# Block sums of the down-projection's weights moved wholly to GpSimd, and the tail's load ring laid over the masked exponentials

## The chip, the cores and the metric

The kernel runs on one core of one Trainium2 chip. Its engines are TensorE (PE, matrix products), VectorE (DVE), ScalarE (ACT), GpSimd (POOL) and SyncE (SP, which here only issues DMAs). Each works through its own list of instructions in order; semaphores join them. The metric is the time of one execution on the device, in microseconds, as the median of several runs.

## The reference

Inputs are x (2048 rows, D = 512), attention weights, the weights of a SwiGLU layer of width F = 1792, and a gate vector. All is float32.

```python
g = sigmoid((x * gate_w).sum(-1, keepdims=True))
# a: 32 heads of 16; a query sees itself and the 255 keys before it
scores = where(mask, q @ k.T * 16 ** -0.5, -1e9)
a = (softmax(scores) @ v).transpose(0, 2, 1, 3).reshape(1, 2048, 512) @ wo
b = (silu(x @ w_gate) * (x @ w_up)) @ w_down
return g * a + (1 - g) * b
```

## The kernel before

**Precision.** A float32 operand is split into a high part (rounded to the type f32r that TensorE reads) and the remainder, the low part; each product is three matmuls (high x high, low x high, high x low). The helper `split` does it: a copy makes the high part, a subtraction (L73) the low part. In the main loop ScalarE mostly makes the high parts (L70) and GpSimd the low ones.

**Main loop.** The attention runs over 8 groups of 4 heads (g) and 16 blocks of 128 positions (i): 128 t-steps, t = 16 g + i, each with four turns hd = 0 to 3, one per head. In a turn TensorE makes a first score product for the row maxima of the next group (L302, reduced by VectorE at L304), a second score product of the present group (L341), whose exponential ScalarE takes (L343), and three steps of the dense projections (`lanes`, L252: gate, up and the next q and k halves). GpSimd masks each pair of exponentials with two selects, L345 and L348, into tiles `pt` of the pool `ptp`. At t%4 == 0, turn 1, the attention product of the four blocks before is made (`av`, L365): it reads the masked `pt` of the step before it. Its result is evicted by ScalarE (L380), transposed and normalised by VectorE, and stored by GpSimd's queue to `od` in DRAM (L395); the tiles of this (`o`) lie in the pool `osb`.

**Order.** There is no automatic scheduler here: the order is written out by hand. `later(t, hd, f)` puts a function into a table AT, and the loop calls what stands at (t, hd) at the end of that turn. The position in this table is the position in the list of the engine that executes it, masks and exponentials of the turn included. SyncE's list holds nearly all loads and stores: the stacked q and k halves, the values (`vg`), weights (`raw`), results kept for later (`kept_h`).

**Block sums.** The down projection runs in the tail in a form with seven block products in place of eight (Winograd's), over the halves of F and of D. It needs four sums of the blocks of the weights `wd`. `sums(k)`, L668 to L693, makes them for k = 0 to 6, once in each of the first seven groups: load two blocks (L674) into a pair of buffers, four additions in place of 128x256 each on GpSimd (L680), two copies 128x512 that make the high parts (L684, ScalarE), two subtractions that make the low parts (L688, GpSimd), and two stores to `sd` in DRAM (L691), which the tail reads. Its inner `at(n, ...)` turns a slot number n, in turns counted from the start of group k, into a place in AT. The pair of buffers comes from `x_pair()`; there is only one pair (bufs=1), which the halves of the next q and k projections (`group_half`, written at L70 by ScalarE and L73 by GpSimd) and the gate (`gate_place`) use in turn. For odd k the next user comes at t+8 of the group.

**Tail.** Behind the loop TensorE makes the last tile of gate and up (`last_tile`, L790; ScalarE's tanh L793 and VectorE make the product), then the output projection of the attention (`mm3`, L88 to L90, with `wo` and `od`) and the seven block products. Loads come through the pool `got` with 10 buffers (`taken`, L757 to L760; L759 issues), split tiles through `hp`, to which the tiles `sg` of the tanh belong. Both pools are opened where `ptp` and `osb` have been closed, in the same memory: pools on the right side grow from that end in the order in which they are opened.

Of the kernel before, what the change touches and what calls it, by code (L numbers as in the profile page):

```python
# [9 lines left out]
F32 = mybir.dt.float32  # L10
# [14 lines left out]
NP = NF // 2  # L25
HD = D // 2
# [10 lines left out]
def gated_mix(ctx, tc, xT, xn, wqk, wv, wo, wgu, wd, gw, outT):  # L37
# [4 lines left out]
    nc = tc.nc  # L42
# [65 lines left out]
    def halves_of(t):  # L108
        n = t.shape[-1] // 2
        return [t[:, :n], t[:, n:]]  # L110
# [43 lines left out]
    sd = dram.tile([4, P, NP, 2, HD], F32, name="sd")  # L154
# [46 lines left out]
    with ExitStack() as A:  # L201
# [19 lines left out]
        def x_pair(pool=None, name="x"):  # L221
            return tuple((pool or sm).tile([P, 2 * CH], F32R, name=f"{name}{w}", bufs=1) for w in ("hi", "lo"))
# [291 lines left out]
        for n, turn in enumerate(turns):  # L514
            for m, _ in enumerate(turn, 3 * NK * n):
                at = [max(0, i - wait) * 2 * NB // (total - wait) for i in (m, m + 1)]
# [19 lines left out]
        def later(t, hd, *fs):  # L536
            AT.setdefault((t, hd), []).extend(fs)

        for n, key in enumerate(KEYS[:-1]):
            if n:  # L540
                t, free = FIRST[key], LAST.get(KEYS[n - 2], 0) + 1 if n > 1 else 0
# [112 lines left out]
        for b in range(NB):  # L654
            t, hd = blocks[b]
            later(t, hd, lambda b=b: gate_block(b))
            if b > 1:
                t, hd = blocks[b - 2]
# [9 lines left out]
        def sums(k):  # L668

            t, buf = k * NB, []  # L670

            def load():
                buf.extend(x_pair())
                nc.sync.dma_start(buf[1].bitcast(F32).rearrange("p (m c) -> p m c", m=2), wd[k:k + NP + 1:NP].rearrange("m p c -> p m c"))  # L674

            def add(m):
                a11, a21, a12, a22 = (buf[1][:, r * HD:(r + 1) * HD].bitcast(F32) for r in range(4))
                to, x, y, op = ((a22, a21, a22, ALU.add), (a21, a11, a21, ALU.subtract),
                                (a11, a22, a11, ALU.subtract), (a12, a12, a11, ALU.subtract))[m]
                nc.gpsimd.tensor_tensor(out=to, in0=x, in1=y, op=op)  # L680

            def high():
                for hi, lo in zip(*map(halves_of, buf)):
                    nc.scalar.copy(hi, lo.bitcast(F32))  # L684

            def low(m):
                hi, lo = (halves_of(t)[m] for t in buf)
                nc.gpsimd.tensor_tensor(out=lo, in0=lo.bitcast(F32), in1=hi.bitcast(F32), op=ALU.subtract)  # L688

            def store(h):  # L690
                nc.sync.dma_start(sd[:, :, k, h].rearrange("j p c -> p j c"),  # L691
                                  buf[h].bitcast(F32).rearrange("p (j c) -> p j c", c=HD))
            def at(n, f, *args):  # L693
                n += 20 + (0 if k % 2 else 3) + (k == NP - 1)
                later(t + n // 4, n % 4, lambda: f(*args))
            later(t + 3, 0, load)
            for m in range(4):
                at(m, add, m)
            at(4, high)
            at(5, store, 0)  # L700
            for m in range(2):
                at(5 + m, low, m)
            at(6, store, 1)

        for k in range(NP):
            sums(k)
# [5 lines left out]
        for t in range(G * NB + 1):  # L712
# [6 lines left out]
            for hd in range(4):  # L719
# [10 lines left out]
                if hd == 1 and part == 0:  # L730
                    if t:
                        ag, c = divmod(d - 1, NCH)
# [11 lines left out]


    with ExitStack() as B:
        hp = B.enter_context(tc.tile_pool(name="hp", bufs=LEAD + 2, side="right"))
        got = B.enter_context(tc.tile_pool(name="got", bufs=10, side="right"))
        wop = B.enter_context(tc.tile_pool(name="wop", bufs=1))

        woh = wop.tile([P, NK, D], F32R, name="woh")
# [2 lines left out]
        def column():  # L754
            return hp.tile([P, CH], F32, name="sg", bufs=4)
# [211 lines left out]
        store = last_tile(0)  # L967
# [15 lines left out]
        store = last_tile(2)  # L983
# [14 lines left out]
        at = {e: n for n, e in enumerate(ITEMS)}  # L998
# [7 lines left out]
        for j in range(2 * NP):  # L1006
            two = divmod(j, 2)
            n = WO + j
# [10 lines left out]
        for n, e in enumerate(ITEMS[:end]):  # L1019
# [13 lines left out]
            p, k, pr = e  # L1033
# [7 lines left out]
        for d in range(2):  # L1041
            t = column()
# [38 lines left out]
```

## Time and profile before

| | |
|---|---|
| median of 3 runs | 829.19 us (828.38 to 829.83) |
| the profiled execution | 835.47 us, its span 833.8 us |
| mean granted clock of TensorE in it | 0.99 |
| busy in the span | PE 810.1, DVE 609.1, ACT 434.2, POOL 378.8 us |

How to read the lines shown below: a timeline row gives start, duration (both us), engine, line of the kernel, operation, output and input by their names in the program, the shapes, and in brackets how long the engine was idle before it and on what. A row of waits gives the engine and instruction that waited, what ended it, the sum in us, how often, and the longest. A row of windows gives a stretch of time, its length, the busy time (and count) of PE, PE's weight loads, DVE, ACT and POOL, then the granted clock as a fraction, the share of the DMA engines' time in use, and GB/s. A group's row gives the count, then the busy sum in us and the mean in ns of one, then the idle time before. Times count from the start of the span.

### The profile page before, as it was taken

The page shows a single profiled execution, that of the slowest core. Times are in us where ns is not written, and L with a number is a line of the kernel's source. Part 1 is how long each engine was busy: PE and PEld are TensorE (multiplying, and loading weights), DVE is VectorE, ACT ScalarE, POOL GpSimd, SP SyncE. Part 2 cuts the span into 40 slices and gives each one's busy share as a digit, 9 for nine tenths or more (in the row PEclk, how much of TensorE's full clock was granted, in tenths as well). Part 3 has the DMA queues.
Part 4 walks back from the last instruction along what each step waited for, and adds up shares of the span by engine and source line. Part 5 has one row for each costly group of instructions (what it writes and reads, how often), then busy time and mean ns, then how long its engine had stood idle before and what let it go on. Part 6 is the DMA issues. An engine that isn't in the chain of part 4 may idle for free. (4 is left out here: it accounts for less than half of the span.)

```text
span 833.8 us, 21474 instructions
## 1 busy us (share of the span) xinstructions
PE 810.1 (97%) x8251; PEld 682.3 (82%) x8251; DVE 609.1 (73%) x1641; ACT 434.2 (52%) x882; POOL 378.8 (45%) x689
## 2 busy tenths in 40 slices
PE   8999999999999999999998999899999989999997
PEld 7888988878878888887887888678887768888886
DVE  5396767768876887787775778786664455898975
ACT  6423556565555566555655566545642323554441
POOL 7722466575556467546656555545640021000112
PEclk9999999999999999999998999999999999999999
DMA  8583525444253364363445416544626699248535
GB/s 290 163 243 118 159 104 143 125 150 146 78 184 103 109 190 149 105 181 115 131 125 165 138 41 203 153 146 141 221 92 208 231 318 328 72 162 265 101 58 95
DMA packets 68378, 130.26 MB, mean 156 GB/s; under 512 B 11124, under 2 KB 23924, under 8 KB 68020
## 3 DMA queue, kind: packets, MB, share of 16 engines
q1 hardware_dynamic: 61172, 107.66, 42.4%
q0 software_dynamic: 7104, 21.24, 8.7%
q8 instruction: 65, 1.06, 0.5%
q14 instruction: 37, 0.30, 0.1%
HBM read 60.16 MB, written 43.53 MB: 124 GB/s over the span
## 5 line engine op out<-in xcount | busy, mean ns | idle before, releaser
L304 DVE CUSTOM_DVE_ANT_0 ps<-ps,mask 128x384 f32<-128x384 f32 (+2 forms) x512 | 268.8, 540 | 113.0 <-PE ps L302 54.8
L343 ACT ACTIVATE pt<-ps 128x384 f32<-128x384 f32 (+2 forms) x512 | 237.3, 474 | 134.5 <-PE ps L302 70.6
L345 POOL TENSOR_SCALAR_AFFINE_SELECT pt<-pt 128x256 f32<-128x256 f32 x256 | 109.8, 430 | 184.0 <-ACT pt L343 182.5
L341 PE MATMUL ps<-q,k 64*128 64x384 f32 (+2 forms) x512 | 162.8, 337 | 11.2 <-ACT pt L343 11.0
L302 PE MATMUL ps<-k,q 63*128 63x384 f32 (+2 forms) x512 | 160.4, 333 | 1.5 <-DVE mx L304 1.5
L252 PE MATMUL pb<-xhi,wh 64*128 64x512 f32 x512 | 117.6, 400 | 0.2
L252 PE MATMUL pb<-xlo,wh 64*128 64x512 f32 x512 | 114.9, 394 | 0.0
L252 PE MATMUL pb<-xhi,wl 64*128 64x512 f32 x512 | 114.7, 394 | 0.0
L252 PE MATMUL pa<-xhi,wh 64*128 64x512 f32 x512 | 114.2, 396 | 0.0
L252 PE MATMUL pa<-xlo,wh 64*128 64x512 f32 x512 | 112.8, 393 | 0.0
L252 PE MATMUL pa<-xhi,wl 64*128 64x512 f32 x512 | 112.6, 393 | 0.0
L341 PEld LDWEIGHTS ps<-q,k 64*128 64x128 f32 x512 | 91.3, 186 | 19.5 <-ACT pt L343 14.9
L302 PEld LDWEIGHTS ps<-k,q 63*128 63x128 f32 x512 | 89.4, 186 | 20.4 <-DVE mx L304 5.8
L348 POOL TENSOR_SCALAR_AFFINE_SELECT pt<-pt 128x256 f32<-128x256 f32 x224 | 95.7, 427 | 0.0
L365 PE MATMUL ps<-pt,vg 64*32 64x320 f32 (+4 forms) x1408 | 75.0, 346 | 0.0
L365 PE MATMUL pb<-pt,vg 64*32 64x320 f32 (+3 forms) x1360 | 73.9, 350 | 0.1
L304 DVE DVE_READ_ACCUMULATOR2_ANT mx<- 128x1 f32 x512 | 71.7, 140 | 0.0
L365 PEld LDWEIGHTS pb<-pt,vg 64*32 64x32 f32 x1360 | 46.4, 106 | 28.4 <-DVE mx L304 5.2
L252 PEld LDWEIGHTS pb<-xhi,wh 64*128 64x128 f32 x512 | 61.2, 187 | 7.0 <-DVE o L382 1.6
L252 PEld LDWEIGHTS pb<-xhi,wl 64*128 64x128 f32 x512 | 61.4, 186 | 5.2
L252 PEld LDWEIGHTS pa<-xhi,wl 64*128 64x128 f32 x512 | 59.3, 185 | 5.8
L252 PEld LDWEIGHTS pa<-xhi,wh 64*128 64x128 f32 x512 | 59.4, 187 | 3.9
(271 smaller groups left out, 1651.1 us busy)
## 6 DMA issues: line engine op xcount, KB each, us to landing
kept_h<-ev SPq DMA_DIRECT2D x52, 256.0 KB
od<-o POOLq DMA_DIRECT2D x32, 256.0 KB, 3.5
raw<-wgu SPq DMA_DIRECT2D x28, 256.0 KB
q<-xhi SPq DMA_DIRECT2D x56, 128.0 KB
k<-xhi SPq DMA_DIRECT2D x56, 128.0 KB
outT<-sg POOLq DMA_DIRECT2D x28, 256.0 KB, 4.7
vd<-vs POOLq DMA_DIRECT2D x8, 672.0 KB, 4.6
vg<-vd SPq DMA_DIRECT2D x32, 168.0 KB
```

What stands on the lines that cost most here:

```text
L252: mm = nc.tensor.matmul(ps[me], w[r], x[r], start=not second and i == 0, stop=bool(second) and i == n - 1)
L302: nc.tensor.matmul(ps[:, :n], QT[g % 2][pr][r, q0:q0 + P], KT[g % 2][pr][r, k0:k0 + n], start=True, stop=True)
L304: mx = nc.vector.tensor_tensor_reduce(out=ps[:, :n], in0=ps[:, :n], in1=mask[:, 3 * P - n:], scale=1.0, scalar=NEG, op0=ALU.add, op1=ALU.m ...
L341: nc.tensor.matmul(ps[:, :n], KT[g % 2][pr][r, k0:k0 + P], QT[g % 2][pr][r, k0:k0 + n], start=True, stop=True)
L343: BEHIND.append(nc.scalar.activation(pt[:, j, :n], ps[:, :n], AF.Exp, scale=SCALE))
L345: nc.gpsimd.affine_select(out=pt[:, :, :P], in_=pt[:, :, :P], pattern=[[0, 2], [1, P]], compare_op=ALU.is_ge, fill=0.0, base=0, channel_mu ...
L348: nc.gpsimd.affine_select(out=pt[:, :, 2 * P:], in_=pt[:, :, 2 * P:], pattern=[[0, 2], [-1, P]], compare_op=ALU.is_ge, fill=0.0, base=-1, ...
L365: nc.tensor.matmul(AV[g, c][h][32 * j:32 * j + 32, q0 - c * CH:q1 - c * CH], VG[4 * g + kb // 4][o, kb % 4, 17 * j:17 * j + 32], PT[g, kb, ...
```

## The change

Three things change. In `sums`, the load and both stores are issued on GpSimd's queue in place of SyncE's, and the two copies are made by GpSimd in place of ScalarE. The table of slots changes with it: additions now start at slot 24 for even k and 22 for odd k (before 23 and 20, one more for the last k), the load four slots ahead of them (before at slot 12), the copies and the first subtraction stand together, each store behind its subtraction. In the tail, `got` is opened ahead of `hp`, so that the loads' ring lies over the memory of the masked exponentials, and the `hp` tiles where the ring's last buffers lay, over `o`.

```diff
@@ -671,7 +671,7 @@
 
             def load():
                 buf.extend(x_pair())
-                nc.sync.dma_start(buf[1].bitcast(F32).rearrange("p (m c) -> p m c", m=2), wd[k:k + NP + 1:NP].rearrange("m p c -> p m c"))
+                nc.gpsimd.dma_start(buf[1].bitcast(F32).rearrange("p (m c) -> p m c", m=2), wd[k:k + NP + 1:NP].rearrange("m p c -> p m c"))
 
             def add(m):
                 a11, a21, a12, a22 = (buf[1][:, r * HD:(r + 1) * HD].bitcast(F32) for r in range(4))
@@ -681,26 +681,27 @@
 
             def high():
                 for hi, lo in zip(*map(halves_of, buf)):
-                    nc.scalar.copy(hi, lo.bitcast(F32))
+                    nc.gpsimd.tensor_copy(hi, lo.bitcast(F32))
 
             def low(m):
                 hi, lo = (halves_of(t)[m] for t in buf)
                 nc.gpsimd.tensor_tensor(out=lo, in0=lo.bitcast(F32), in1=hi.bitcast(F32), op=ALU.subtract)
 
             def store(h):
-                nc.sync.dma_start(sd[:, :, k, h].rearrange("j p c -> p j c"),
-                                  buf[h].bitcast(F32).rearrange("p (j c) -> p j c", c=HD))
+                nc.gpsimd.dma_start(sd[:, :, k, h].rearrange("j p c -> p j c"),
+                                    buf[h].bitcast(F32).rearrange("p (j c) -> p j c", c=HD))
+
             def at(n, f, *args):
-                n += 20 + (0 if k % 2 else 3) + (k == NP - 1)
+                n += 22 + 2 * (k % 2 == 0)
                 later(t + n // 4, n % 4, lambda: f(*args))
-            later(t + 3, 0, load)
+            at(-4, load)
             for m in range(4):
                 at(m, add, m)
             at(4, high)
-            at(5, store, 0)
             for m in range(2):
-                at(5 + m, low, m)
-            at(6, store, 1)
+                at(4 + m, low, m)
+            for h in range(2):
+                at(5 + h, store, h)
 
         for k in range(NP):
             sums(k)
@@ -744,8 +745,8 @@
 
 
     with ExitStack() as B:
+        got = B.enter_context(tc.tile_pool(name="got", bufs=10, side="right"))
         hp = B.enter_context(tc.tile_pool(name="hp", bufs=LEAD + 2, side="right"))
-        got = B.enter_context(tc.tile_pool(name="got", bufs=10, side="right"))
         wop = B.enter_context(tc.tile_pool(name="wop", bufs=1))
 
         woh = wop.tile([P, NK, D], F32R, name="woh")
```

On GpSimd, at the block sum k=2, from the last addition to the pair of masks whose end the attention product at t=40 awaits. Before (`pt` are the masked exponentials, `wl` the low part of a projection's weights):

```order
L680 TENSOR_TENSOR xlo<-xlo 128x256
L345 AFFINE_SELECT pt<-pt 128x2x128
L348 AFFINE_SELECT pt<-pt 128x2x128
L688 TENSOR_TENSOR xlo<-xlo,xhi 128x512
L73 TENSOR_TENSOR wl<-raw,wh 128x512
L345 AFFINE_SELECT pt<-pt 128x2x128
L348 AFFINE_SELECT pt<-pt 128x2x128
L688 TENSOR_TENSOR xlo<-xlo,xhi 128x512
L345 AFFINE_SELECT pt<-pt 128x2x128
L348 AFFINE_SELECT pt<-pt 128x2x128
```

After:

```order
L680 TENSOR_TENSOR xlo<-xlo 128x256
L684 CAST xhi<-xlo 128x512 x2
L688 TENSOR_TENSOR xlo<-xlo,xhi 128x512
L73 TENSOR_TENSOR wl<-raw,wh 128x512
L345 AFFINE_SELECT pt<-pt 128x2x128
L348 AFFINE_SELECT pt<-pt 128x2x128
L688 TENSOR_TENSOR xlo<-xlo,xhi 128x512
L691 DMA sd<-xhi 128x4x256
L691 DMA sd<-xlo 128x4x256
L345 AFFINE_SELECT pt<-pt 128x2x128
L348 AFFINE_SELECT pt<-pt 128x2x128
```

Two copies have come ahead of the subtractions and two stores behind them, all ahead of the awaited pair, the last row of both.

On GpSimd, at the block sum k=1, up to the masks that the attention product at t=24 awaits and the next write to the buffers (`xlo<-ev,xhi`). Before:

```order
L348 AFFINE_SELECT pt<-pt 128x2x128
L688 TENSOR_TENSOR xlo<-xlo,xhi 128x512
L395 DMA od<-o_1347 128x512
L688 TENSOR_TENSOR xlo<-xlo,xhi 128x512
L345 AFFINE_SELECT pt<-pt 128x2x128
L348 AFFINE_SELECT pt<-pt 128x2x128
L345 AFFINE_SELECT pt<-pt 128x2x128
L348 AFFINE_SELECT pt<-pt 128x2x128
L345 AFFINE_SELECT pt<-pt 128x2x128
L348 AFFINE_SELECT pt<-pt 128x2x128
L73 TENSOR_TENSOR xlo<-ev,xhi 128x512
```

After:

```order
L684 CAST xhi<-xlo 128x512 x2
L688 TENSOR_TENSOR xlo<-xlo,xhi 128x512
L345 AFFINE_SELECT pt<-pt 128x2x128
L348 AFFINE_SELECT pt<-pt 128x2x128
L688 TENSOR_TENSOR xlo<-xlo,xhi 128x512
L691 DMA sd<-xhi 128x4x256
L691 DMA sd<-xlo 128x4x256
L345 AFFINE_SELECT pt<-pt 128x2x128
L348 AFFINE_SELECT pt<-pt 128x2x128
L345 AFFINE_SELECT pt<-pt 128x2x128
L348 AFFINE_SELECT pt<-pt 128x2x128
L73 TENSOR_TENSOR xlo<-ev,xhi 128x512
```

Copies and stores stand here among the masks too; the next write to the buffers follows two pairs of masks behind the stores, where it followed three pairs behind the last subtraction.

On SyncE at the start of the tail (DMAHW and DMASW are completions of transfers by issuing queue, the latter GpSimd's). Before, then after:

```order
L581 DMA kept_h<-ev 128x512 [waits DVE_49]
L581 DMA kept_h<-ev 128x512 [waits DMAHW3_49,DVE_49]
L759 DMA got<-wo 128x512 [waits DMASW6_49,DMASW7_49,DMASW5_49,DMAHW0_49,DMASW4_49,DMAHW2_49,DMASW3_49,DMAHW3_49,DMASW2_49,DMAHW4_49,DMASW1_49,DMAHW5_49,DMASW0_49,DMAHW6_49,DVE_49,DMAHW7_49,Activation_49,Pool_49]
L759 DMA got<-wo 128x512 x3
L877 DMA k_10706<-gd 128x2048
```

```order
L581 DMA kept_h<-ev 128x512 [waits DVE_49]
L581 DMA kept_h<-ev 128x512 [waits DMAHW6_49,DVE_49]
L760 DMA got<-wo 128x512 [waits DMAHW7_49,PE_49,Pool_49]
L760 DMA got<-wo 128x512 [waits DMAHW0_49]
L760 DMA got<-wo 128x512 [waits DMAHW1_49]
```

The first load of `wo` waited for all queues of transfers and three engines; now for one transfer, TensorE and GpSimd. On ScalarE at the same place, before and after:

```order
L380 COPY o_1348<-ps_10625 128x512 [waits PE_49]
L793 ACTIVATE sg<-pa 128x512 [waits PE_49,Pool_49]
L70 CAST woh<-got 128x512 [waits DMASW7_49,DMASW6_49,DMAHW0_49,DMASW5_49,DMAHW2_49,DMASW4_49,DMAHW3_49,DMASW3_49,DMAHW4_49,DMASW2_49,DMAHW5_49,DMASW1_49,DMAHW6_49,DMASW0_49,DMAHW7_49,DVE_49,Activation_49]
L70 CAST woh<-got 128x512 [waits DMAHW5_49]
L793 ACTIVATE sg<-pa 128x512 [waits PE_49]
```

```order
L380 COPY o_1345<-ps_10625 128x512 [waits PE_49]
L794 ACTIVATE sg<-pa 128x512 [waits DMASW6_49,DMASW5_49,DMASW7_49,DMASW4_49,DMAHW0_49,DMASW3_49,DMAHW1_49,DMASW2_49,DMAHW2_49,DMASW1_49,DMAHW3_49,DMASW0_49,DMAHW5_49,DVE_49,DMAHW6_49,PE_49,DMAHW7_49,Activation_49,Pool_49]
L70 CAST woh<-got 128x512 [waits DMAHW7_49]
L70 CAST woh<-got 128x512 [waits DMAHW0_49]
L794 ACTIVATE sg<-pa 128x512 [waits PE_49]
```

The list of transfers stands at the first tanh (`sg<-pa`) now, where it stood at the split of the first `wo` tile.

## The prediction

> **What bounds the kernel now.** I read the page first, then the waits, then the times at which the output of each attention block is evicted.
>
> ```profile
> PE 810.1 (97%) x8251; PEld 682.3 (82%) x8251; DVE 609.1 (73%) x1641; ACT 434.2 (52%) x882; POOL 378.8 (45%) x689
> ```
>
> ```profile
> PE ps L341 <- ACT pt L343: 11.0, 7, 3.1
> ...
> ACT xhi L684 <- POOL xlo L680: 9.6, 12, 2.1
> ```
>
> TensorE (PE) sets the time: 810 of 833.8 us. What can be won is the time in which it does not work at its pace, and the only large group of such idle time in the main loop is seven waits of the second score product (L341) for ScalarE's exponential (L343). There are seven block sums, and ScalarE (ACT) waits 9.6 us in the copies of L684 for GpSimd's (POOL's) additions; its exponentials stand behind them. The recorded idle time is not all that is lost, since ends of matmuls are modelled. A better ruler is the spacing of the evictions of the attention product (L380, one in four t-steps; rows give start, duration, engine, line):
>
> ```profile
> 97.23 0.54 ACT L380 COPY o<-ps 128x448 f32<-128x448 f32 x1 [2.16 <-PE ps L365]
> ...
> 117.75 0.59 ACT L380 COPY o<-ps 128x512 f32<-128x512 f32 x1 [2.68 <-PE ps L365]
> ...
> 166.78 0.53 ACT L380 COPY o<-ps 128x448 f32<-128x448 f32 x1 [2.16 <-PE ps L365]
> 185.58 0.59 ACT L380 COPY o<-ps 128x512 f32<-128x512 f32 x1 [1.74 <-PE ps L365]
> ...
> 235.39 0.53 ACT L380 COPY o<-ps 128x448 f32<-128x448 f32 x1 [2.13 <-PE ps L365]
> 254.22 0.59 ACT L380 COPY o<-ps 128x512 f32<-128x512 f32 x1 [2.69 <-PE ps L365]
> 270.91 0.59 ACT L380 COPY o<-ps 128x512 f32<-128x512 f32 x1 [1.61 <-PE ps L365]
> 287.23 0.59 ACT L380 COPY o<-ps 128x512 f32<-128x512 f32 x1 [2.21 <-PE ps L365]
> ...
> 438.61 0.53 ACT L380 COPY o<-ps 128x448 f32<-128x448 f32 x1 [2.16 <-PE ps L365]
> 461.39 0.59 ACT L380 COPY o<-ps 128x512 f32<-128x512 f32 x1 [1.74 <-PE ps L365]
> ...
> 529.13 0.59 ACT L380 COPY o<-ps 128x512 f32<-128x512 f32 x1 [1.31 <-PE ps L365]
> ```
>
> A clean interval is 16.3 (270.91 to 287.23); the one after a 448-wide eviction I put at 16.7, since that product is shorter by a part that I estimate at 0.4. The intervals with a block sum are 20.5 (k=0), 18.8 (k=1), 18.8 (k=2) and 22.8 (k=5); read the same way, k=3, 4 and 6 are 17.8, 18.8 and 18.6. Over 16.7 that is 19.2 us in all, and the following intervals lose 5.5 more (0.4 at 254.22 to 270.91), so **24.7 us** are lost around the seven sums. Some 5 of them are a halved clock:
>
> ```profile
> 110.00:120.00 10.00, 9.93 (x147) 8.16 (x145) 6.00 (x21) 4.22 (x10) 5.13 (x10) 0.83 0.35 115
> 440.00:450.00 10.00, 6.93 (x63) 5.64 (x63) 6.99 (x24) 5.17 (x11) 6.55 (x12) 0.93 0.38 121
> 450.00:460.00 10.00, 9.95 (x95) 9.08 (x103) 3.75 (x12) 5.90 (x13) 7.49 (x14) 0.72 0.53 177
> ```
>
> The column behind the five engines is the granted clock: 0.07 and 0.28 of 10 us make 3.5 us lost behind the longest stall (k=5), 0.17 makes 1.7 us at k=0.
>
> **The change in the main loop, even k.** ScalarE loses its fourteen copies and with them its wait. GpSimd, in order, gains two copies and three DMA issues per sum, and between them stand the masks (L345, L348) that the attention product at t+8 reads. So the question is when the last mask of t+7 ends.
>
> ```profile
> 248.46 1.28 POOL L73 TENSOR_TENSOR wl<-raw,wh 128x512 fp32r<-128x512 f32 x1 [0.66 <-ACT wh L70]
> ...
> 252.03 0.41 POOL L348 TENSOR_SCALAR_AFFINE_SELECT pt<-pt 128x256 f32<-128x256 f32 x1
> ...
> 528.16 0.42 POOL L348 TENSOR_SCALAR_AFFINE_SELECT pt<-pt 128x256 f32<-128x256 f32 x1
> ```
>
> At k=2 it ends at 252.44, with 0.66 idle in the ten us before it: GpSimd is already full. At k=6 the mask at 528.16 was the one awaited, and its eviction came 0.55 after its end (529.13). An undisturbed k=2 eviction is due at 235.39 + 16.7 = 252.1, so the mask is due at 251.5.
>
> No copy stands on GpSimd before. Bounds from the rows:
>
> ```profile
> L73 POOL TENSOR_TENSOR wl<-raw,wh 128x512 fp32r<-128x512 f32 x33 | 42.4, 1285 | 23.6 <-ACT wh L70 23.6
> ...
> L395 POOL DMA_DIRECT2D od<-o x32 | 17.9, 559 | 9.3 <-DVE o L394 8.4
> ...
> L443 POOL DMA_DIRECT2D vd<-vs x8 | 7.4, 922 | 31.6 <-ACT vs L440 31.6
> ...
> L211 POOL TENSOR_SCALAR_AFFINE_SELECT mask<-mask 128x384 f32<-128x384 f32 x1 | 0.5, 505 | 0.1
> ```
>
> At most it is the two-input subtraction, 1.29 us; at least the one-input select of 384 columns, 0.50. I take 0.6, the select's rate carried on to 512 columns, since both read one tile. An issue costs 0.56 to 0.92; I take 0.6, the 128x512 store. The chain becomes 252.44 + 2 x 0.6 (copies) + 2 x 0.6 (stores) + 0.3 (what remains of the load's issue ahead of it) - 0.66 (idle filled) = 254.5, 3.0 behind its due time; with 0.2 in the next interval **3.2** per even k, where k=2 loses 2.5 now. ScalarE's stall is gone, but TensorE waits for masks in its place, at L365. k=6 keeps another 2.1 in its second interval, where a fetch for the gate stands that the change leaves alone.
>
> The Trainium skill (GPSIMD Engine Reference, 3.1 Elementwise) gives 1.8 cycles per element at 1.2 GHz for a tight one-input loop, an estimate of 0.77 us for 512; no run shows it for a copy yet. By that the even k would lose 0.3 us more each.
>
> **Odd k.** The sum starts when its load has landed:
>
> ```profile
> 164.95 0.38 SPq L674 DMA_DIRECT2D xlo<-wd  x1
> ```
>
> ```profile
> 170.90 0.74 POOL L680 TENSOR_TENSOR xlo<-xlo 128x256 f32<-128x256 f32 x1 [1.53 <-issue]
> ...
> 182.26 0.40 POOL L348 TENSOR_SCALAR_AFFINE_SELECT pt<-pt 128x256 f32<-128x256 f32 x1
> ```
>
> From issue to landing 5.95 us. GpSimd now reaches the load's slot (t+4, third head) at about 165, the same moment, so the additions begin at 171 again; one pair of masks (0.72) then lies ahead of them, and the last mask ends at 182.66 - 0.72 + 1.2 + 1.2 + 0.25 = 184.6, due 183.5 - 0.55 = 182.9. But something else is later. The buffer is wanted at t+8 by the next halves of X, and ScalarE must write the first one there:
>
> ```profile
> 181.84 0.61 ACT L70 CAST xhi<-ev 128x512 fp32r<-128x512 f32 x1
> ```
>
> ```profile
> 185.48 0.44 PE L341 MATMUL ps<-q,k 64*128 64x384 f32 x1
> ```
>
> ```profile
> DMA to landing us min/median/max: 2.3/3.5/4.4
> ```
>
> The store of xhi is issued 0.6 + 0.6 + 2 x 0.72 before the last mask's end, at 182.0, and lands (as the 128x512 stores of od, 2.3 to 4.4) at 184.3 to 186.4; I take 185.3. Behind it come the cast 0.6, an eviction 0.6 and the exponential 0.5, so 187.0. The product that reads it began at 185.48, undisturbed 183.4 (less the 2.1 of its interval): some 3.6, with the follow-up **4.0** for k=1 and 3, which lose 2.8 and 1.7 now. For k=5 the load takes longer today:
>
> ```profile
> 437.12 0.38 SPq L674 DMA_DIRECT2D xlo<-wd  x1
> ```
>
> ```profile
> 444.13 0.92 POOL L680 TENSOR_TENSOR xlo<-xlo 128x256 f32<-128x256 f32 x1 [2.94 <-DMA kept_h<-ev]
> ```
>
> The addition reads that load (the profile names another transfer as the releaser). 7.0 in place of 5.95, so 4.0 + 1.2 = 5.2 there, in place of 6.6.
>
> Sum: 4 x 3.2 + 2.1 + 2 x 4.0 + 5.2 = 28.1. Stalls of 3 to 5 us in one piece will often halve the clock; the rows give 1.7 to 3.5 for one. I count four of seven at 1.7: 6.8. So 34.9 in place of 24.7, **+10.2**. By the low bounds (copies 0.5, stores 0.56, a load from GpSimd landing in 3.5, so that the chain starts some 1.2 earlier, stores in 2.3, no halved clock) an even k loses 1.3, an odd one 1.8 and k=5 3.5: with the gate's 2.1 that is 14.4, or -10.3. By the high ones (0.3 per store and 0.7 per copy more, 2.0 on each of seven sums, 1.7 of clock at all seven) 28.1 + 14.0 + 11.9 = 54.0, or +29.
>
> **The tail.** SyncE's first load of wo lies over the memory of o, and waits for the last store of od:
>
> ```profile
> SPq L759 <- DMA od<-o: 7.3, 1, 7.3
> ```
>
> ```profile
> 630.74 1.76 SPq L759 DMA_DIRECT2D got<-wo  x4
> ```
>
> ```profile
> 626.49 0.60 ACT L793 ACTIVATE sg<-pa 128x512 f32<-128x512 f32 x1 [1.84 <-PE pa L790]
> ```
>
> ```profile
> 627.91 0.56 POOL L395 DMA_DIRECT2D od<-o  x1 [2.37 <-DVE o L394]
> ```
>
> Over the masked exponentials it waits only for the last attention product, evicted from 624: loads start some 7 us earlier. What TensorE loses to their lateness:
>
> ```profile
> 630.00:640.00 10.00, 10.00 (x46) 8.29 (x45) 3.87 (x6) 3.36 (x6) 0.00 (x0) 1.00 0.74 250
> 640.00:650.00 10.00, 8.65 (x37) 6.58 (x37) 5.17 (x10) 3.93 (x7) 0.00 (x0) 1.00 0.84 260
> ...
> 670.00:680.00 10.00, 7.69 (x26) 5.57 (x25) 6.46 (x10) 2.96 (x5) 2.36 (x5) 0.83 0.98 309
> ```
>
> A full window holds 46 matmuls. 37 and 26 mean 2.0 and 4.3 us lost, 6.3 in all. In exchange the tiles of the tanh (L793) now lie over o: the first, at 626.49, waits until od has landed, 630.2 at the least (627.91 + 2.3) and 632.3 at the most. Its bank of PSUM is wanted by the third column chunk,
>
> ```profile
> 634.38 0.39 PE L790 MATMUL pa<-xhi,wh 128*128 128x512 f32 x1
> ```
>
> and behind the landing come tanh and product, 1.3: it costs nothing to 1 us. The window at 670 is also full of transfers (0.98), of which part stays. I take **-5.0**; bounds -6.3 and 0, the latter if the store, not the load, is what everything waits for.
>
> **Net.** 835.5 (profiled) + 10.2 - 5.0 = 840.7. The profiled execution is 6.3 above the median of the runs, so the median becomes **834**.
>
> **Rivals.**
> A: GpSimd is cheap enough. Halfway from 28.1 without halved clocks (+3.4) to the low bound (-10.3) is -3.5; with the tail 835.5 - 3.5 - 5.0 - 6.3 = **821**. For it: its loads go past SyncE's queue, and the select's rate; against: 0.66 us of idle time in ten. It decides if a sum adds under 1 us to GpSimd's chain. This is the other side of my forecast.
> A2: the change does all it could: ScalarE's 11.0 and the 5.1 of clock go, and nothing comes for them: 835.5 - 11.0 - 5.1 - 5.0 - 6.3 = **808**. Against: GpSimd is late already.
> B: gain and loss cancel. One halved clock and not four gives 28.1 + 1.7 = 29.8, +5.1, against -5.0 in the tail: **829**.
> C: the clock halves at each stall. Seven at 2.6 (between 1.7 and 3.5) make 18.2 for my 6.8: **845**. For it: the k=5 and k=0 rows; against: most of the seven waits pass without a drop today. The Trainium skill (TensorE: Matmul & The Clock Gate, Why this matters for your kernels) warns of gaps over some 3 us; the rows agree for k=5 (longest wait 3.1), and by that rule my stalls stand on the edge.
>
> **How the numbers follow.** Forecast 0.42 (its own range 831 to 838), A 0.22, A2 0.07, B 0.13, C 0.16. A measurement here tells 0.2%, 1.7 us. Faster is A and A2, 0.29; same is B, 0.13; slower 0.58. The range leaves out A2 and the outer ends of A and C: 819 to 845.
>
> **What would show it.** Intervals of L380: about 19.9 in even k, 18 to 19 and a longer one behind it in odd k. TensorE waiting at L365 for masks of GpSimd in even k, ScalarE's cast of X (L70) waiting for the store of sd in odd k; no L684 on ScalarE. SyncE's first load of wo right behind 624, full windows where 37 matmuls were, the first tanh waiting for od. Wrong I am if the copy on GpSimd takes under 0.5 or over 0.9 us, if its load lands in under 4, or if GpSimd's masks are not awaited at all.

## The result

The changed kernel takes 855.8 us (855.0 to 858.5, 4 runs) against 828.8 us for the kernel before (824.9 to 829.8, 4 runs): a ratio of 1.034, with a 95% interval of 1.030 to 1.038. It is 27 us slower. The direction was forecast; the size (834, a range to 845) was not. Here and below, executions in a slow state are left out of times and ratios: one of e7 (909.2 us at a granted clock of 0.84), one of e9 (983.1 at 0.75), and one of the kernel before (2026.8). The ratios of the experiments go by executions of the kernel before that were made along with them (medians of 828.4 to 829.5 us).

The profiled execution took 855.14 us, its span 853.4. The page's first row and the waits that answer to those of before (engine, instruction and what ended the wait; sum in us, how often, longest):

```profile
PE 814.5 (95%) x8251; PEld 681.5 (80%) x8251; DVE 608.6 (71%) x1641; ACT 425.8 (50%) x868; POOL 402.7 (47%) x724
```

```profile
PE pb L365 <- ACT ev L591: 20.2, 3, 8.3
ACT xhi L70 <- DMA sd<-xhi: 19.6, 3, 8.1
PE pa L252 <- POOL wl L73: 9.9, 4, 2.8
...
POOL xlo L680 <- DMA xlo<-wd: 6.9, 6, 3.3
```

The wait of the score product L341 for an exponential (11.0 us, seven times) is gone, and so is ScalarE's wait for the additions. In their place are three waits of the attention product (L365) for an eviction on ScalarE, 20.2 us, and four waits of a projection (L252) for the low part of its weights, which GpSimd makes, 9.9 us. Three and four: the odd and the even block sums.

The evictions of the attention product, in the timeline of ScalarE, for k=0, 1, 2 and 5:

```profile
97.28 0.53 ACT L380 COPY o<-ps 128x448 f32<-128x448 f32 x1 [2.16 <-PE ps L365]
...
118.37 0.59 ACT L380 COPY o<-ps 128x512 f32<-128x512 f32 x1 [4.14 <-PE ps L365]
...
167.38 0.53 ACT L380 COPY o<-ps 128x448 f32<-128x448 f32 x1 [2.16 <-PE ps L365]
...
191.98 0.59 ACT L380 COPY o<-ps 128x512 f32<-128x512 f32 x1 [3.79 <-PE ps L365]
...
241.56 0.53 ACT L380 COPY o<-ps 128x448 f32<-128x448 f32 x1 [2.13 <-PE ps L365]
...
264.09 0.59 ACT L380 COPY o<-ps 128x512 f32<-128x512 f32 x1 [5.05 <-PE ps L365]
...
458.12 0.53 ACT L380 COPY o<-ps 128x448 f32<-128x448 f32 x1 [2.16 <-PE ps L365]
...
485.10 0.59 ACT L380 COPY o<-ps 128x512 f32<-128x512 f32 x1 [3.79 <-PE ps L365]
```

The intervals are 21.1 (k=0), 24.6 (k=1), 22.5 (k=2) and 27.0 (k=5). All seven of both kernels and of the experiments below, read in the same way, with the time from the last eviction to the end of the span:

| kernel | k=0 | 1 | 2 | 3 | 4 | 5 | 6 | first to last eviction | behind it |
|---|---|---|---|---|---|---|---|---|---|
| before | 20.5 | 18.8 | 18.8 | 17.8 | 18.8 | 22.8 | 18.6 | 526.8 | 209.7 |
| changed | 21.1 | 24.6 | 22.5 | 24.6 | 20.9 | 27.0 | 20.6 | 550.5 | 205.7 |
| e1: pools of the tail alone | 19.0 | 20.7 | 18.8 | 18.3 | 18.8 | 21.7 | 18.6 | 527.0 | 208.9 |
| e2: block sums alone | 21.1 | 25.8 | 20.4 | 24.6 | 20.1 | 25.6 | 21.1 | 548.9 | 205.9 |
| e3: all transfers on SyncE | 18.9 | 18.9 | 20.2 | 20.0 | 20.2 | 21.6 | 18.7 | 528.7 | 208.5 |
| e4: copies on ScalarE | 21.0 | 21.7 | 22.3 | 21.0 | 20.8 | 22.7 | 18.9 | 537.8 | 206.8 |
| e5: stores on SyncE | 19.5 | 19.0 | 22.0 | 19.0 | 19.5 | 22.1 | 19.5 | 530.3 | 205.3 |
| e6: load on SyncE | 19.4 | 24.2 | 20.2 | 24.7 | 19.2 | 25.1 | 20.3 | 542.1 | 209.0 |
| e7: store of xhi first (its second profile) | 23.3 | 20.9 | 24.2 | 21.6 | 24.4 | 22.8 | 22.2 | 550.3 | 206.0 |
| e8: filled wait | 21.1 | 22.3 | 20.0 | 24.7 | 20.2 | 22.7 | 20.8 | 541.8 | 208.5 |
| e9: three pools in the tail | 20.6 | 18.0 | 18.8 | 18.1 | 20.4 | 19.2 | 20.8 | 526.1 | 203.4 |
| e10: spread slots | 16.8 | 17.7 | 16.7 | 17.4 | 16.6 | 19.2 | 19.0 | 516.3 | 205.1 |
| e11: both | 16.8 | 17.4 | 16.7 | 18.2 | 16.7 | 18.4 | 18.6 | 515.9 | 203.3 |

Each row is one execution, and a single interval is a coarse ruler. The loop of the changed kernel is also that of e2, and that of the kernel before also that of e1 and e9; between these an interval moves by up to 2.1 us in the one (k=2) and 3.6 in the other (k=5). The granted clock differs there: at k=2 it fell in the changed kernel (0.83 and 0.82 in the windows from 250 to 270) and not in e2. The part behind the loop moves by four with the old order of the pools (209.7, 205.9 and 205.1 in before, e2 and e10), and by as much with the new one (205.3 to 209.0 in changed, e1 and e3 to e8). The profiled executions of e4 and e5 are the fastest of their kernels (843.4 against a median of 847.0, 834.0 against 840.8). TensorE's waits are steadier: the wait for an eviction that is explained below sums to 20.2 us in the changed kernel and 20.5 in e2, the wait for the low part of a weight to 9.9, 10.3 and 10.0 in the changed kernel, e2 and e8.

**Odd k.** At k=1, GpSimd's timeline up to the awaited masks, ScalarE's, and TensorE's:

```profile
178.50 1.17 POOL L684 CAST xhi<-xlo 128x512 fp32r<-128x512 f32 x2
179.63 1.29 POOL L688 TENSOR_TENSOR xlo<-xlo,xhi 128x512 fp32r<-128x512 f32 x1
...
182.82 0.78 POOL L691 DMA_DIRECT2D sd<-xhi  x1
183.60 0.76 POOL L691 DMA_DIRECT2D sd<-xlo  x1
...
185.44 0.40 POOL L348 TENSOR_SCALAR_AFFINE_SELECT pt<-pt 128x256 f32<-128x256 f32 x1
```

```profile
179.96 0.49 ACT L343 ACTIVATE pt<-ps 128x384 f32<-128x384 f32 x1 [0.38 <-PE ps L341]
186.19 0.62 ACT L70 CAST xhi<-ev 128x512 fp32r<-128x512 f32 x1 [5.74 <-DMA sd<-xhi]
186.72 0.58 ACT L591 COPY ev<-pb 128x512 f32<-128x512 f32 x1
```

```profile
187.35 0.74 PE L365 MATMUL pb<-pt,vg 64*32 64x320 f32 x1 [5.93 <-ACT ev L591]
```

The store of xhi goes out at 182.8, and ScalarE goes on 3.4 us later, when it has landed. ScalarE stands at the cast into the same buffer from 180.4 to 186.2. Behind the cast stands the eviction of a projection's bank `pb`, and the attention product needs that bank. So TensorE stops at the attention product itself, with 5.93 us idle, and starts it at half pace: 0.74 us a matmul, where e8 below has 0.45.

**Even k.** At k=2, in the same order:

```profile
248.92 0.74 POOL L680 TENSOR_TENSOR xlo<-xlo 128x256 f32<-128x256 f32 x1 [1.11 <-DMA xlo<-wd]
...
253.71 1.16 POOL L684 CAST xhi<-xlo 128x512 fp32r<-128x512 f32 x2
254.84 1.25 POOL L688 TENSOR_TENSOR xlo<-xlo,xhi 128x512 fp32r<-128x512 f32 x1
256.06 1.25 POOL L73 TENSOR_TENSOR wl<-raw,wh 128x512 fp32r<-128x512 f32 x1
...
259.23 0.79 POOL L691 DMA_DIRECT2D sd<-xhi  x1
```

```profile
257.37 0.79 PE L252 MATMUL pa<-xhi,wl 64*128 64x512 f32 x2 [2.77 <-POOL wl L73]
```

GpSimd waits 1.1 us for the load to land ahead of the first addition. Then two copies and a subtraction stand ahead of `wl`, and TensorE, in order, waits 2.77 us for it at L252. The masks come later than that, and no wait of the attention product for them is recorded in this execution.

**Clock.** Windows of the changed kernel (clock behind the five engines, as before):

```profile
180.00:190.00 10.00, 4.07 (x62) 2.11 (x66) 1.11 (x4) 2.45 (x5) 8.25 (x14) 0.75 0.27 107
...
330.00:340.00 10.00, 6.94 (x114) 4.43 (x116) 1.66 (x6) 4.25 (x9) 5.00 (x9) 0.66 0.22 88
...
470.00:480.00 10.00, 2.14 (x20) 1.50 (x16) 1.61 (x6) 1.50 (x4) 8.98 (x16) 0.76 0.47 175
```

In this execution the clock halves at all three odd sums; in the windows of the even ones (110, 250 and 260, 400, 550) it is down to 0.82 or 0.83.

**Tail.** The order of the waits turned as expected, but not their length:

```profile
647.39 2.90 SPq L760 DMA_DIRECT2D got<-wo  x4
```

```profile
651.60 0.56 POOL L395 DMA_DIRECT2D od<-o  x1 [2.37 <-DVE o L394]
```

```profile
659.15 0.60 ACT L794 ACTIVATE sg<-pa 128x512 f32<-128x512 f32 x1 [10.82 <-DMA got<-wd]
```

The loads start right behind the last attention product. The first tanh, which waits for the store of od, starts 7.5 us after that store is issued. The profile names a later transfer as the releaser; but in this run and in the seven experiments that have the tanh over o as well (e1 and e3 to e8) the tanh starts 0.6 to 0.7 us behind the slowest landing of these stores, here 6.9 us.

### The profile page after: what moved, and what is told of

The parts are those of the page before. It is cut to its first block, busy times and chain, and to the rows that moved or that the text cites. A ratio compares the mean times of both kernels' runs of the same rounds, so it can differ in the third digit from the quotient of the medians.

```text
span 853.4 us, 21516 instructions
## 1 busy us (share of the span) xinstructions
PE 814.5 (95%) x8251; PEld 681.5 (80%) x8251; DVE 608.6 (71%) x1641; ACT 425.8 (50%) x868; POOL 402.7 (47%) x724
## 4 chain that ended last, share of the span: by engine, by line
PE 80%; POOL 8%; DMA 7%; DVE 2%; issue 2%; SPq 1%; ACT 1%; POOLq 0%; ACTq 0%
PE pa L252 19%; PE pb L252 18%; PE pb L365 7%; PE ps L302 5%; PE ps L88 4%; PE ps L90 4%; DMA xlo<-wd 4%; PE ps L89 4%; PE ps L341 3%; POOL xlo L680 2%; PE pb L232 2%; PE pa L232 2%; PE pb L90 2%; PE pa L90 2%; PE pb L89 2%
## 5 line engine op out<-in xcount | busy, mean ns | idle before, releaser
L341 PE MATMUL ps<-q,k 64*128 64x384 f32 (+2 forms) x512 | 161.5, 334 | 0.0
L252 PE MATMUL pa<-xhi,wl 64*128 64x512 f32 x512 | 111.7, 399 | 9.9 <-POOL wl L73 9.9
L252 PE MATMUL pb<-xhi,wh 64*128 64x512 f32 x512 | 113.4, 395 | 0.2 <-DVE o L382 0.2
L252 PE MATMUL pa<-xhi,wh 64*128 64x512 f32 x512 | 112.3, 397 | 0.0
L252 PE MATMUL pb<-xlo,wh 64*128 64x512 f32 x512 | 111.8, 391 | 0.0
L252 PE MATMUL pb<-xhi,wl 64*128 64x512 f32 x512 | 111.7, 391 | 0.0
L252 PE MATMUL pa<-xlo,wh 64*128 64x512 f32 x512 | 111.0, 394 | 0.0
L365 PE MATMUL pb<-pt,vg 64*32 64x320 f32 (+3 forms) x1360 | 84.4, 388 | 20.2 <-ACT ev L591 20.2
L302 PEld LDWEIGHTS ps<-k,q 63*128 63x128 f32 x512 | 89.2, 186 | 18.2 <-issue 6.3
L341 PEld LDWEIGHTS ps<-q,k 64*128 64x128 f32 x512 | 90.9, 185 | 5.7 <-issue 0.8
L365 PEld LDWEIGHTS pb<-pt,vg 64*32 64x32 f32 x1360 | 49.2, 116 | 56.8 <-ACT ev L591 21.5
L365 PE MATMUL ps<-pt,vg 64*32 64x320 f32 (+4 forms) x1408 | 85.5, 382 | 0.0
L252 PEld LDWEIGHTS pa<-xhi,wl 64*128 64x128 f32 x512 | 57.3, 187 | 18.0 <-POOL wl L73 11.6
L252 PEld LDWEIGHTS pb<-xhi,wh 64*128 64x128 f32 x512 | 58.6, 185 | 6.6 <-DVE o L382 0.9
L938 POOL DMA_DIRECT2D outT<-sg x14 | 11.9, 849 | 109.5 <-DVE sg L933 109.5
L252 PEld LDWEIGHTS pb<-xhi,wl 64*128 64x128 f32 x512 | 58.5, 184 | 5.3
```

The lines of the kernel that those rows point to most:

```text
L252: mm = nc.tensor.matmul(ps[me], w[r], x[r], start=not second and i == 0, stop=bool(second) and i == n - 1)
L302: nc.tensor.matmul(ps[:, :n], QT[g % 2][pr][r, q0:q0 + P], KT[g % 2][pr][r, k0:k0 + n], start=True, stop=True)
L341: nc.tensor.matmul(ps[:, :n], KT[g % 2][pr][r, k0:k0 + P], QT[g % 2][pr][r, k0:k0 + n], start=True, stop=True)
L365: nc.tensor.matmul(AV[g, c][h][32 * j:32 * j + 32, q0 - c * CH:q1 - c * CH], VG[4 * g + kb // 4][o, kb % 4, 17 * j:17 * j + 32], PT[g, kb, ...
```

## The experiments

### The two parts apart

e1 swaps the pools of the tail alone, in the kernel before; e2 leaves that swap out of the changed kernel:

```diff
+        got = B.enter_context(tc.tile_pool(name="got", bufs=10, side="right"))
         hp = B.enter_context(tc.tile_pool(name="hp", bufs=LEAD + 2, side="right"))
-        got = B.enter_context(tc.tile_pool(name="got", bufs=10, side="right"))
```

> The kernel before with the two pools of the tail swapped and nothing else. Theory (the swap wins what the traces of the two kernels show behind the last eviction of the attention product, 209.7 before and 205.7 after): 4 us less than before, about 825. Rival (the tail's gain needs the other part, since in the changed kernel fewer transfers are pending on SyncE at that point): 0 to 2 us less, 827 to 829.

> The changed kernel with the two pools of the tail in their old order, so the block sums' part alone. Theory (the two parts add up): 855.8 + 4 = 860, which is 31 over before; the seven intervals with a block sum as in the changed kernel (20.6 to 27.0). Rival (the tail gains more with the sums changed): 856 to 858.

Measured: e1 830.2 us, a ratio of 1.000 (0.996 to 1.004) to the kernel before; e2 854.1 us, 1.031 (1.026 to 1.036). Neither theory on the tail holds: the block sums carry the whole loss, and the swap moves nothing that these runs can tell (the ratio's interval is 3 us to either side). In e1's tail TensorE stands for this (waits, and the store):

```profile
ACT sg L793 <- DMA got<-od: 12.3, 1, 12.3
...
PE pa L790 <- DVE sg L794: 3.6, 1, 3.6
```

```profile
628.45 0.56 POOL L395 DMA_DIRECT2D od<-o  x1 [2.37 <-DVE o L394]
```

```profile
637.45 0.60 ACT L793 ACTIVATE sg<-pa 128x512 f32<-128x512 f32 x1 [12.26 <-DMA got<-od]
```

```profile
DMA to landing us min/median/max: 2.3/3.2/8.4
```

The tanh starts 9.0 us after the issue, and the landings of od over the whole of that run (last row) go up to 8.4 us, where they ended at 4.4 before. The swap is what makes the store land late: the slowest landing is 4.4 to 5.3 us in the three profiles with the old order (before, e2, e10) and 6.0 to 8.5 in the ten with the new one. With the new order SyncE's loads start ahead of this store; how they hold it up was not tried apart.

### Which of the moved steps costs

e3 issues the load and both stores on SyncE again, e4 makes the copies on ScalarE again, e5 moves back the stores alone, e6 the load alone; slots and the rest stay as changed:

```diff
-                nc.gpsimd.dma_start(buf[1].bitcast(F32).rearrange("p (m c) -> p m c", m=2), wd[k:k + NP + 1:NP].rearrange("m p c -> p m c"))
+                nc.sync.dma_start(buf[1].bitcast(F32).rearrange("p (m c) -> p m c", m=2), wd[k:k + NP + 1:NP].rearrange("m p c -> p m c"))
...
-                    nc.gpsimd.tensor_copy(hi, lo.bitcast(F32))
+                    nc.scalar.copy(hi, lo.bitcast(F32))
...
-                nc.gpsimd.dma_start(sd[:, :, k, h].rearrange("j p c -> p j c"),
+                nc.sync.dma_start(sd[:, :, k, h].rearrange("j p c -> p j c"),
```

The first piece is in e3 and e6, the second in e4, the third in e3 and e5.

> The changed kernel with the load and the two stores of the block sums issued on SyncE again, slots as changed, copies on GpSimd. Theory (odd k waits for the store of xhi, which stands in GpSimd's list behind the first subtraction; even k waits for the low part of a weight, wl, behind the copies): the store goes out when the copies end, some 3 us earlier, so the intervals of k=1, 3, 5 fall by 3.5 or more (24.6 to about 20.5, 27.0 to about 22), those of even k stay within 1 us; about 842. Rival (GpSimd's list is simply too full, by 2.3 us of issues per sum): all seven intervals fall alike, by 2 to 3 us; about 840.

> The changed kernel with the two copies made by ScalarE again, slots as changed, transfers on GpSimd. Theory: GpSimd's list gets 1.2 us shorter per sum, but the subtraction then waits for ScalarE and ScalarE for the additions, as before the change; odd k still wait for the store of xhi, 0.6 us earlier: about 850, 5 us less than the changed kernel. Rival (GpSimd too full): 1.2 us and part of the halved clock back at each sum, 843 to 846.

> The changed kernel with the two stores of the block sums back on SyncE and the load left on GpSimd. With all three transfers back it took 833.7, 22 less than the changed kernel. Theory (the stores carry the loss: the one of xhi stands in GpSimd's list behind the first subtraction and a pair of masks, so it lands late for odd k, and both issues of 0.78 hold masks up): 836 to 840, odd intervals 19 to 21.5. Rival (the load carries it, since the first addition waits for it on GpSimd with masks behind it): 850 or more.

> The changed kernel with the load of the block sums back on SyncE and the stores left on GpSimd. Theory (the stores carry the loss): 850 to 854, odd intervals still 23.5 or more. Rival (the load carries it): 836 to 840.

Measured, as ratios to the kernel before: e3 833.7 us, 1.007 (1.004 to 1.010); e4 847.0, 1.021 (1.017 to 1.025); e5 840.8, 1.013 (1.010 to 1.017); e6 849.7, 1.023 (1.019 to 1.028).

With the transfers back on SyncE 22 of the 27 us are gone, although the copies stay on GpSimd: the transfers carry most of the cost. The copies and the later slots, which e3 keeps, leave some 5 us; these two were not tried one without the other. e3 is 6 to 8 us faster than its theory and its rival said. The odd intervals fall by 4.6 to 5.7, as the theory had it, but the even ones fall too, by 0.7 to 2.3, which it had excluded. e5 and e6 part the two. The stores carry the odd sums: 24.6, 24.6, 27.0 become 19.0, 19.0, 22.1 with them on SyncE, and stay at 24.2 to 25.1 when only the load goes back. For the even sums the intervals do not decide, since e2 has 20.4 and 20.1 at k=2 and 4 with everything on GpSimd, but the waits do. In e5, and then in e6:

```profile
PE pa L252 <- POOL wl L73: 10.4, 4, 3.4
...
PE pb L365 <- ACT ev L591: 8.5, 3, 3.9
...
ACT xhi L70 <- POOL xlo L688: 7.9, 3, 3.7
```

```profile
PE pb L365 <- ACT ev L591: 18.1, 3, 6.5
...
PE pa L252 <- POOL wl L73: 7.0, 4, 1.8
```

Of the 9.9 us of TensorE's wait for `wl` the load makes 3; the stores, which stand behind `wl`, make none. The other 7.0 are in e3 too. The even intervals of e5 are shorter all the same by 0.5 to 1.6, and the windows go with that: among the even sums its clock fell at k=2 alone, where that of the changed kernel fell at all four. Of the odd wait the stores make 12 us. What is left of it in e5 is no longer the store: ScalarE's cast into the buffer then waits for the second subtraction (L688), which reads that buffer too.

e5's 840.8 is just above its theory's range, e6's 849.7 just below. e4 gave more than its theory: the odd intervals fell by 2.9 to 4.3 for 1.2 us less in GpSimd's list, and its 847.0 lies 1 us above the rival's range. In e4's waits ScalarE stands for the additions again and TensorE for exponentials, while the attention product's wait has fallen from 20.2 to 5.2:

```profile
PE ps L341 <- ACT pt L343: 15.9, 7, 3.8
ACT xhi L684 <- POOL xlo L680: 13.2, 14, 2.1
...
PE pb L365 <- ACT ev L591: 5.2, 3, 2.5
```

So a list that is too full is part of it, as the rival said, but its price differs by place.

### The place of the store

e7 keeps every instruction on GpSimd and moves the store of xhi ahead of the first subtraction:

```diff
             at(4, high)
+            at(4, store, 0)
             for m in range(2):
                 at(4 + m, low, m)
-            for h in range(2):
-                at(5 + h, store, h)
+            at(6, store, 1)
```

> The changed kernel with the store of xhi put directly behind the two copies in GpSimd's list, ahead of the first subtraction; same engine, same count of instructions. Theory (odd k waits for that store, so its place counts): it is issued 2 us earlier (1.25 subtraction, 0.72 masks), so odd intervals fall by 2 or more; even ones gain 0.8, since wl now stands behind the issue; 850 to 853. Rival (the landing of a GpSimd store near other transfers, or the number of issues, sets the wait): odd intervals move by less than 1; 856.

> The kernel with the store of xhi directly behind the copies once more, for a profile, since its time (854.3) was nearer to no change than to the 3 to 5 us expected. Theory (place of the store counts): TensorE's waits for ScalarE's eviction ahead of the attention product (20.2 us in the changed kernel) about halve, odd intervals near 22.5, and even intervals grow, because wl stands behind the issue. Rival: odd intervals stay at 24 and more.

Measured: 853.9 us (three executions), 1.028 (1.024 to 1.032), and 855.1 in the run for the profile. From the time alone one would say that the place does not matter. The waits of the profile say otherwise:

```profile
PE pa L252 <- POOL wl L73: 16.6, 4, 5.0
...
PE pb L365 <- ACT ev L591: 11.4, 3, 4.6
...
ACT xhi L70 <- POOL xlo L688: 10.8, 3, 4.4
```

The odd wait falls from 20.2 to 11.4, and the odd intervals by 3.0 to 4.2, more than the 2 us that the store moved. As in e5, what ScalarE's cast waits for is now the second subtraction (last row), so a still earlier store would win nothing there. The even wait grows from 9.9 to 16.6, and the even intervals by 1.7 to 3.5, two to four times the 0.8 us of one issue. The two cancel. What makes the even side so steep was not tried apart; at k=2 the trace has, besides the issue, 0.3 us in which it waits for the copies to end, and 0.8 more in which GpSimd waits for the load.

### The clock

e8 fills the wait of the odd sums with work that nothing uses: 24 matmuls into a bank that the attention product then overwrites.

```diff
+            if g % 2 and c == 1 and g < G - 1:
+                for n in range(24):
+                    nc.tensor.matmul(AV[g, c][1], KT[g % 2][0][0:64, :P], QT[g % 2][0][0:64, :CH], start=True, stop=True)
             orders = [[4 * c + m for m in ms
```

> The changed kernel with 24 extra matmuls (64x128 by 512, into the bank that the attention product then overwrites) ahead of the attention product at t+8 of k=1, 3, 5, where TensorE otherwise waits 5.9 to 8.3 us. They are extra work of some 5.3 us in a wait. Theory (the wait halves the clock, and the halved clock adds 2 us or more to each of these intervals): the product takes 2.3 and not 4.2 us, intervals of k=1, 3 fall from 24.6 to about 22.5, that of k=5 by 1 to 2; about 850. Rival (the product is slow for another reason, such as its operands): no change, 856, or more by what the extra matmuls outlast the wait.

Measured: 850.2 us, 1.024 (1.020 to 1.028): more work, and 5.6 us less than the changed kernel. At k=1:

```profile
181.21 5.61 PE L361 MATMUL ps<-q,k 64*128 64x512 f32 x24
...
187.02 0.45 PE L368 MATMUL pb<-pt,vg 64*32 64x320 f32 x1 [0.20 <-ACT ev L594]
```

```profile
180.00:190.00 10.00, 9.80 (x138) 7.50 (x136) 1.11 (x5) 2.82 (x6) 8.24 (x14) 1.00 0.27 107
```

The attention product starts nearly when it does in the changed kernel (187.0 and 187.35), but at full pace: from its start to that of its eviction it takes 2.59 us, where it took 4.63. That is the price of the clock apart from the wait: 2.0 us of the 2.3 by which the interval falls. k=5 falls from 27.0 to 22.7. There the product takes 2.59 in place of 4.63 as well, so again 2.0 are the clock; the rest is a shorter wait (GpSimd waited 0.7 us for that load in this run, 3.3 in the changed kernel). k=3 did not move. There 0.93 us of idle time were left behind the fill, and the clock halved all the same:

```profile
328.65 0.64 PE L368 MATMUL pb<-pt,vg 64*32 64x320 f32 x1 [0.93 <-ACT ev L594]
```

```profile
330.00:340.00 10.00, 10.00 (x145) 8.58 (x131) 6.29 (x21) 5.08 (x11) 5.69 (x11) 0.89 0.14 34
```

Even sums stayed at full clock at times without any fill (k=2: 20.0). So the forecast of 850 was met in part by luck: k=3 gave nothing, k=5 more than its clock, and of the 8.7 us by which the loop is shorter some 3 are even sums that the fill does not touch.

### A version faster than both

Three readings point the same way: GpSimd is crowded for some ten microseconds per sum but busy for only 6 tenths of the loop as a whole (311 of 530 us in the kernel before), even sums have time until t+12, and the tanh need not lie over o. e9 gives the tanh's tiles a pool between `got` and `hp`; e10 spreads the slots, with engines and queues as before the change (for odd k the copies, subtractions and stores stand one turn later); e11 does both.

```diff
-        hp = B.enter_context(tc.tile_pool(name="hp", bufs=LEAD + 2, side="right"))
         got = B.enter_context(tc.tile_pool(name="got", bufs=10, side="right"))
+        sgp = B.enter_context(tc.tile_pool(name="sgp", bufs=4, side="right"))
+        hp = B.enter_context(tc.tile_pool(name="hp", bufs=LEAD + 2, side="right"))
...
-            return hp.tile([P, CH], F32, name="sg", bufs=4)
+            return sgp.tile([P, CH], F32, name="sg")
```

```diff
-                n += 20 + (0 if k % 2 else 3) + (k == NP - 1)
+                n += 20 if k % 2 else 24
...
+            step = 2 if k in (0, 2, 4) else 1
             for m in range(4):
-                at(m, add, m)
+                at(step * m, add, m)
-            at(4, high)
-            at(5, store, 0)
+            late = {1: k % 2, 2: 0}[step] + 4 * step
+            at(late, high)
+            at(late + 1, store, 0)
             for m in range(2):
-                at(5 + m, low, m)
-            at(6, store, 1)
+                at(late + step + m * step, low, m)
+            at(late + 2 * step, store, 1)
```

> The kernel before with the two pools of the tail swapped and the tiles of the tanh in a pool of their own between them, so that they too lie over the masked exponentials and only the split tiles lie over o. The swap alone moved nothing measurable (ratio 1.0002). Theory (the swap starts the loads 7 us earlier, and the first tanh, which then waits for the store of od, gives the same time back): with the tanh freed, 3 to 5 us less than before, 824 to 826. Rival (the start of the tail is not what holds the tail up; its loads come in at the rate of the transfers anyway): within 1.5 us of before, 827 to 830.

> The kernel before, engines and queues as before, with the slots of the block sums spread: for k=0, 2, 4 the additions and subtractions stand two turns apart (the buffers are not wanted before t+12 there), and for k=1, 3, 5 the copies stand one turn later on ScalarE. Theory (what the block sums cost is GpSimd's crowding over some ten us, in which ScalarE or TensorE then waits; GpSimd has room in the group as a whole): the intervals of k=0, 2, 4 fall from 20.5, 18.8, 18.8 to 16.7 to 17.5, the odd ones by up to 1; 6 to 9 us less than before, 820 to 823. Rival (the sums cost by their sum of work on GpSimd, wherever it stands): within 2 us of before.

> Both edits, the spread slots and the three pools of the tail, on the kernel before. Theory: they add up, 815 to 819. Rival (the tail takes back what the loop wins, or the other way round): no better than the better one of the two.

Measured: e9 827.2 us, a ratio of 0.997 (0.995 to 1.000); e10 822.0, 0.992 (0.989 to 0.996); e11 818.8, 0.989 (0.985 to 0.992). e11 is the fastest kernel of this study, 10 us under the kernel before. e9's 2 us lie between the differences that the theory and the rival gave, and its 827.2 in the rival's range. The wait that the tanh made in e1 (3.6 us) is gone from its list. In its profile TensorE has no idle time in the windows from 620 to 690, and the part behind the last eviction is 203.4 us, 203.3 in e11: the two shortest seen, against 205 to 210 in all the others. In e10 the intervals of k=0, 2 and 4 fall to 16.6 to 16.8, which is what was taken for undisturbed; 0.9 us of it move to the next interval. The odd ones fall by 0.4 to 3.6, but the 19.2 of k=5 stands in e9 too, where the loop is as before. The clock is at 1.00 in every window of 10 us from 90 to 620 in e10 and e11. Both parts add up: 2.1 and 7.3 us less apart, 10.5 together. What is left on TensorE in e11's waits:

```profile
PE ps L341 <- ACT pt L343: 2.8, 3, 1.7
...
PE pb L365 <- ACT ev L591: 1.6, 3, 0.6
```

## Why the prediction was wrong

**Right:** the direction, and part of its reason. GpSimd had no room in the ten us ahead of the attention product, its list got longer, and TensorE's wait for exponentials was replaced by others. The odd sums wait for the store of xhi through ScalarE's in-order list. The copy costs what was taken: two in 1.17 us, 0.6 each, and not the 0.77 of the estimate given beside it. An issue, taken at 0.6, cost 0.74 to 0.79. Halved clocks matter.

**Odd sums, the step that failed most.** "so 187.0. The product that reads it began at 185.48, undisturbed 183.4": I followed ScalarE's list to the exponential and asked which product reads that. Between cast and exponential I counted "an eviction 0.6", without asking whose bank it frees. It is the bank of the attention product, which stands one turn earlier. TensorE therefore stopped at 181.4, not at 183.4, and none of the 2.3 us of that product covered the wait. The landing, at 186.2, was 0.9 us later than I took, since the store went out 0.8 later; the 3.4 us from its issue to the cast are about as I had them. The halved product came on top. (At k=5 the surcharge of 1.2 for the slower load should have been 1.05 by its own figures.) Forecast 4.0, 4.0 and 5.2 us lost without clocks, 13.2 in all; found, clocks included, 26.1 over the clean 16.7 and 1.9 in the next intervals.

**Even sums.** The step "the question is when the last mask of t+7 ends" looked at the wrong one of GpSimd's readers. `wl` stands ahead of those masks in the quoted list, and TensorE needs it first. The wait for masks at L365 that I gave as a sign did not come. The load was "0.3" in my sum, for its issue alone; at k=2 GpSimd waited another 1.1 for it to land, and by e6 it makes 3 of the 9.9 us that TensorE waits in the four. Forecast 14.9 us for the four without clocks, 18.8 with four sevenths of the 6.8; found, clocks included, 18.3 and 1.9. So the size was nearly right by luck, for another wait. (The low bound of 1.3 per even k comes out at 1.7 from the terms named with it.)

**Clock.** I counted four halvings of 1.7. In the profiled execution all seven sums halved it, and e8 measured 2.0 us for those at k=1 and k=5. That was rival C's condition; C's time (845) still missed by 11, since it kept the odd sums' short wait. The waits of 5.9 to 8.3 us in the odd sums were each followed by a halved clock; in e8 0.93 us at k=3 was too, and 0.60 at k=5 was not. The Trainium skill (TensorE: Matmul & The Clock Gate, Why this matters for your kernels) warns of gaps over some 3 us between bursts of matmuls. The odd sums of the changed kernel agree, but the 0.93 us show that the length of one gap does not decide alone here.

**Tail.** "-5.0" came from a landing of "2.3 to 4.4", read where the transfers were not crowded. With the loads let go ahead of it the same store landed after 6.9 us in the changed kernel and 8.4 in e1, and the tanh, which I had costed at up to 1 us, held TensorE 2.1 us in the one and 3.6 in the other. By its ratio the swap alone changes the time by 0.2 us (between -3.1 and +3.5). Also, the 6.3 us that I wanted back are not lost in each execution: e2 and e10 with the old order are 4 us shorter behind the loop than the profile I read them from.

**Sum.** 5.2 us forecast, 27 found. Main loop +10.2 forecast and +23.6 between first and last eviction: about 12 of the missing 13 are the odd sums, if my four halved clocks are shared out over the seven. The other 8 are not parted cleanly. By e1 the tail's five did not come, though the two profiled tails differ by 4.0. And I took 6.3 us off because the profiled execution was above the median; that held for the kernel before alone: the changed kernel's profiled execution is 0.7 below its median.

By the medians the load on GpSimd costs 6 us and the stores 15 (e6 and e5 against the changed kernel), together 22 (e3). The profiled loops give 8 and 20, but that of e5 is its fastest execution.

## What to carry to other kernels

When an instruction on an in-order engine gets a later wait, list everything that stands behind it and the resource that each one frees, banks too, and price the wait at the earliest of their readers. Do the same for the buffer that is waited for: behind the store stood a second reader. A store that guards a buffer belongs where its data is ready and on a queue that has nothing to do; behind compute work its issue is as late as that work. Before moving work from one engine to another to end a crowd, look at whether it can be spread over time: here that gave 0.8%, where moving it cost 0.7% with the transfers left in their place (e3) and 3.4% with them.

## What was not expected of the hardware

- The slowest landing of a 128x512 store from GpSimd was 4.4 to 5.3 us in the three profiles where SyncE's loads wait for that store, and 6.0 to 8.5 us in the ten where they had been let go ahead of it.
- Issues of the sums' transfers (512 KB, several rows of DRAM per partition) took GpSimd 0.74 to 0.79 us each, the store of od (256 KB) 0.56.
- Filling waits of 5.9 us and more with useless matmuls kept the clock up at two of three places, and the product behind the wait then took 2.59 us in place of 4.63.
